# A linear-attention, routed-experts and gated-output kernel: weight sums of a later stage issued one per step over four buffers, without copies kept for the general path, and row loads ahead of weight loads

## The chip, the cores and the metric

The kernel runs on one core of a Trainium2 chip. The metric is device time in microseconds (us) of one execution; lower is better. The time of a kernel is the median of several executions. Beside it stands one profiled execution, whose trace is what the rows below are taken from. The engines are named as in the profile: PE is TensorE (matmuls, with PEld for its weight loads), DVE is VectorE, ACT is ScalarE, POOL is GpSimd, and SP issues most of the transfers (SPq is its queue).

## What is computed

The reference chains three parts, all in fp32:

```python
def _attn_ref(q, k, v, f_logit):            # (4, 8, 768, 48) each
    f = 1.0 / (1.0 + np.exp(-f_logit))
    for t in range(S):
        state = f[:, :, t, :, None] * state + np.einsum('bhd,bhe->bhde', k[:, :, t], v[:, :, t])
        y[:, :, t] = np.einsum('bhd,bhde->bhe', q[:, :, t], state)
def _moe_ref(x, expert_emb, tau, w1, w2):   # x (3072, 384), 8 experts, F = 1024
    expert_idx = np.argmax(xn @ en.T / tau, axis=1)   # xn, en: normalised rows
    gate_w = probs[np.arange(N), expert_idx]
    for e in range(E):
        h = np.maximum(x[mask] @ w1[e], 0.0)
        out[mask] = gate_w[mask, None] * (h @ w2[e])
def _moe2_ref(x, w_a, w_b, w_out):          # (384, 1536), (384, 1536), (1536, 384)
    return ((x @ w_a) * (x @ w_b) @ w_out).astype(np.float32)
```

## The kernel before

It has three stages on one core. **Attention** runs up to about 135 us: chunks of the recurrence, then the routing, which scatters each token's row into a DRAM buffer `slots`, sorted by expert. The **experts** run from there to about 404 us, the **gated output** from there to the end.

Matmuls are made of pairs: an fp32 value is split into a rounded part (hi, fp32r) and the rest (lo), and three matmuls (hi·hi, lo·hi, hi·lo) stand for one exact product. So each weight has to be split on the way: ScalarE copies the hi part, then GpSimd or VectorE subtracts it from the raw value.

**The experts' loop** has 64 steps s, 8 for each expert e (j = s % 8). A step does 128 of the 1024 hidden columns: `h_part(s)` is the first matmul (L1205 to L1207, into `ph`), then ScalarE's `hh` (L1228, relu) and VectorE's `hl` (L1229); `y_part(s - 1)` is the second matmul of the step before (L1248, into `po`), in thirds hi·`hh`, lo·`hh`, hi·`hl`. In steps j = 3, 4, 5 TensorE transposes the next expert's rows (`x_turn`, L1195, into `pt`), which come with one load from `slots` (`rows_load`, L464; for expert 1 into a tile that the trace calls `yT`, for the later ones `rows`). Raw expert weights come in pieces of 768 KB (L131 for the first ones, L879 after) and are split by `job_run`: ScalarE L887 or L893, then three subtractions of 512 columns, two on GpSimd (L896) and one on VectorE. `w_more` starts a piece when it was loaded at least `LAG_N` = 2 steps ago and its place in the ring of weights is free.

**Side work in the same steps** readies the gated stage. `prep_run(s, us)` first issues what `defer` put down for this step, then `loads()`, then as much of its streams as a budget of `us` allows (1.1 in the first eight steps, 1.8 after):

- `conv`: the weights of the gated stage, `moe2_w_a`, `moe2_w_b` (w = 0, 1) and `moe2_w_out` (w = 2), come as raw 8-byte words in 18 blocks (L926, 768 KB each, into `part` buffers 3, 4, 5 of the tile `big`). Bit operations turn each into fp32: ScalarE L949 into `ct`, then VectorE L951 to L958. Blocks of `moe2_w_out` are also split and stored in DRAM, `wost` (L970).
- `combine(w)`: for `moe2_w_a` and then `moe2_w_b`, the gated stage multiplies with 15 sums of 384 x 512 blocks' parts rather than with the weights. First three stores put the whole matrix aside in DRAM, `wkeep` (L1000), from where only the general path (`general`, taken when a flag is set, which it isn't here) reads it. Then for each of 15 sums: up to two VectorE operations (L1002, L1003); a step later ScalarE's hi (L1028) into one of nh = 3 + w buffers `hilo` and the lo (L1031) on GpSimd if the sum had operations, else on VectorE at the end of the step's side work; another step later the store into `wst` (L1047). A buffer is taken again `can` = 3 steps after its sum. Several sums of a step are possible as long as budget and buffers allow: sums 3, 3, ... at a time.
- `w_chunk`: the first three loads of `wst` back into SBUF (L1066) close the loop.

**The gated output** visits chunks of `wst` (`visit`, matmuls L1453 into `pv` and `pw`), adds the products up on VectorE (L1463, L1469), multiplies and splits (L1430, L1434, L1435) and multiplies with `w_out` (L1482 to L1486), whose blocks `wo_load` brings from `wost` (L1425) three iterations ahead. The last blocks of `moe2_w_out` are converted in this stage.

The order on each engine is the order in which the Python issues; every engine works its own list off in order. SP's list holds all the loads and stores named here, so a transfer that waits on SP holds up those behind it.

## Time and profile before

| | us |
|---|---|
| median of 3 executions (838.61 to 839.34) | 838.92 |
| the profiled execution, its own time | 843.84 |
| span of its trace, first to last instruction | 842.0 |

| engine | busy us | share of the span |
|---|---|---|
| TensorE matmul (PE) | 777.7 | 92% |
| TensorE weight load (PEld) | 743.7 | 88% |
| VectorE (DVE) | 609.2 | 72% |
| ScalarE (ACT) | 420.9 | 50% |
| GpSimd (POOL) | 392.1 | 47% |

The mean granted clock of TensorE is 0.976 of full speed; the transfers move 231.54 MB, 275 GB/s over the span. Busy time is the time in which an engine works on an instruction; the shares are means over stages with different limits, so the table of stretches below is read with them. In the rows, "idle before" in square brackets is how long an engine had nothing to do ahead of an instruction and what released it.

### The profile page before, as it was taken

How to read it: one execution, taken by the hardware profiler on the slowest of the kernel's cores; microseconds unless marked ns; L12 is line 12 of the kernel's file. 1: busy time of each engine (PE TensorE's matmuls, PEld its weight loads, DVE VectorE, ACT ScalarE, POOL GpSimd, SP SyncE). 2: the span in 40 equal slices, each digit the busy share in tenths (PEclk: the TensorE clock that was granted, in tenths of full speed). 3: DMA queues.
4: the chain of work that ended last, by engine and by line, in shares of the span. 5: the costliest groups of instructions: out<-in, count | busy, mean ns of one | idle time of the engine just before them, and what ended most of it. 6: DMA issues, size and time to landing. Idle time of an engine off the chain costs nothing. (4 is left out here: it accounts for less than half of the span.)

```text
span 842.0 us, 16799 instructions
## 1 busy us (share of the span) xinstructions
PE 777.7 (92%) x6354; PEld 743.7 (88%) x6354; DVE 609.2 (72%) x1019; ACT 420.9 (50%) x889; POOL 392.1 (47%) x380
## 2 busy tenths in 40 slices
PE   7899989599988899889878999999999999999995
PEld 5899988588887898889868999999999999999995
DVE  7999985389978767678677766756765786676552
ACT  5899963366546455374434444434433443444331
POOL 6667762253535463384044336415535343532413
PEclk9999999799999989989999999999999999999999
DMA  7989733967699885997987889889889979888982
GB/s 263 317 291 341 245 130 122 252 195 267 213 314 298 240 262 180 309 231 215 350 333 268 291 311 339 305 293 337 305 289 314 330 284 317 333 296 306 340 302 72
DMA packets 83903, 231.54 MB, mean 275 GB/s; under 512 B 10697, under 2 KB 42295, under 8 KB 77543
## 3 DMA queue, kind: packets, MB, share of 16 engines
q1 hardware_dynamic: 80455, 220.81, 78.2%
q0 software_dynamic: 3072, 9.56, 2.9%
q8 instruction: 52, 0.85, 0.4%
q14 instruction: 36, 0.29, 0.1%
q10 hardware_dynamic: 288, 0.02, 0.0%
HBM read 192.95 MB, written 37.42 MB: 274 GB/s over the span
## 5 line engine op out<-in xcount | busy, mean ns | idle before, releaser
L1435 POOL TENSOR_TENSOR w<-big,w 128x512 fp32r<-128x512 f32 x72 | 96.4, 1354 | 194.8 <-ACT w L1434 182.3
L1453 PE MATMUL pv<-w,w 128*128 128x256 f32 x912 | 136.7, 285 | 11.0 <-DVE big L1469 6.1
L1469 DVE TENSOR_TENSOR big<-big,pv 128x512 f32<-128x512 f32 x144 | 98.3, 683 | 62.5 <-PE pv L1453 62.4
L1453 PEld LDWEIGHTS pv<-w,w 128*128 128x128 f32 x912 | 127.5, 190 | 15.0 <-DVE big L1469 8.6
L1453 PE MATMUL pv<-a,w 128*128 128x256 f32 x816 | 120.6, 282 | 0.3
L1453 PEld LDWEIGHTS pv<-a,w 128*128 128x128 f32 x816 | 113.8, 189 | 2.4 <-DVE big L1469 1.2
L896 POOL TENSOR_TENSOR w<-raw,w 128x512 fp32r<-128x512 f32 x48 | 76.7, 1626 | 60.4 <-ACT w L893 56.5
L1248 PE MATMUL po<-hh,w 128*128 128x224 f32 (+7 forms) x384 | 84.0, 355 | 17.0 <-ACT hh L1228 16.4
L1486 PE MATMUL pq<-raw,w 128*128 128x384 f32 x288 | 97.6, 339 | 1.0 <-POOL w L1435 1.0
L1482 PE MATMUL pq<-raw,w 128*128 128x384 f32 x288 | 97.5, 338 | 0.0
L1484 PE MATMUL pq<-raw,w 128*128 128x384 f32 x288 | 97.1, 337 | 0.0
L1248 PEld LDWEIGHTS po<-hh,w 128*128 128x128 f32 x384 | 68.8, 196 | 20.5 <-ACT hh L1228 18.2
L1463 DVE TENSOR_TENSOR big<-big,pv 128x256 f32<-128x256 f32 x96 | 40.3, 420 | 52.9 <-PE pv L1453 49.7
L1205 PE MATMUL ph<-a,w 128*128 128x224 f32 (+7 forms) x192 | 66.9, 349 | 0.0
L1206 PE MATMUL ph<-a,w 128*128 128x224 f32 (+7 forms) x192 | 66.8, 348 | 0.0
L1207 PE MATMUL ph<-a,w 128*128 128x224 f32 (+7 forms) x192 | 66.7, 347 | 0.0
L1430 DVE TENSOR_TENSOR big<-big 128x512 f32<-128x512 f32 x72 | 64.1, 917 | 1.6
L1434 ACT ACTIVATE w<-big 128x512 fp32r<-128x512 f32 x72 | 44.8, 633 | 39.5 <-DVE big L1430 39.5
L1460 ACT ACTIVATE big<-pw 128x256 f32<-128x256 f32 x48 | 18.4, 383 | 77.8 <-PE pw L1453 77.8
L1486 PEld LDWEIGHTS pq<-raw,w 128*128 128x128 f32 x288 | 54.5, 189 | 1.6 <-POOL w L1435 1.6
L1482 PEld LDWEIGHTS pq<-raw,w 128*128 128x128 f32 x288 | 54.4, 189 | 0.3 <-ACT w L1434 0.3
L1484 PEld LDWEIGHTS pq<-raw,w 128*128 128x128 f32 x288 | 54.5, 189 | 0.0
(275 smaller groups left out, 1706.2 us busy)
## 6 DMA issues: line engine op xcount, KB each, us to landing
w<-wst SPq DMA_DIRECT2D x49, 1024.0 KB
w<-wst SPq DMA_DIRECT2D x49, 896.0 KB
raw<-wost SPq DMA_DIRECT2D x72, 384.0 KB
raw<-moe_w SPq DMA_DIRECT2D x32, 768.0 KB
qkf<-qkf SPq DMA_DIRECT2D x20, 768.0 KB
wst<-big SPq DMA_DIRECT2D x24, 512.0 KB
vx<-vx SPq DMA_DIRECT2D x24, 192.0 KB
big<-moe_w_out SPq DMA_DIRECT2D x6, 768.0 KB
```

Of the source, the lines that this page charges most:

```text
L896: (G if i < NPOOL else V).tensor_tensor(out=wt[:, 1, f], in0=raw[:, f], in1=wt[:, 0, f].bitcast(F32), op=ALU.subtract)
L1205: T.matmul(out=out, lhsT=wh, rhs=xh, start=first, stop=False)
L1206: T.matmul(out=out, lhsT=wl, rhs=xh, start=False, stop=False)
L1207: T.matmul(out=out, lhsT=wh, rhs=xl, start=False, stop=last)
L1248: T.matmul(out=OS[e][k], lhsT=w[:, j % 4, k * 128:(k + 1) * 128], rhs=x, start=(j == 0 and w is wh and x is hh), stop=(j == FJ - 1 and x i ...
L1430: V.tensor_tensor(out=a, in0=a, in1=b, op=ALU.mult)
L1435: G.tensor_tensor(out=g[:, 1], in0=a, in1=g[:, 0].bitcast(F32), op=ALU.subtract)
L1453: T.matmul(out=out, lhsT=wt, rhs=xt_, start=first and j == 0, stop=j == 2, skip_group_check=True)
L1469: V.tensor_tensor(out=o, in0=o, in1=bank, op=ALU.subtract)
L1482: T.matmul(out=q, lhsT=gh, rhs=wh, start=(f == 0), stop=False)
L1484: T.matmul(out=q, lhsT=gh, rhs=wl, start=False, stop=False)
L1486: T.matmul(out=q, lhsT=gl, rhs=wh, start=False, stop=(f == F2J - 1))
```

## The change

The text below gives the change's names; apart from the general path it touches the side work, the raw weights' lag, the order of some loads, and `wo_load`.

- No copy is kept in `wkeep`: its six stores (three for each matrix, 768 KB each) are gone. `general` recomputes the two matrices from the inputs by the same bit operations.
- `combine` has four buffers for both matrices. For the first one the fourth isn't `hilo[3]` but two pieces of `big` (columns 1024 to 1536 of each of its first two parts), and its store goes out in two cuts. A buffer is taken again after four steps. After each sum a `yield None` ends the stream's work for the step, so there is at most one sum in a step. The lo subtraction is on GpSimd for 14 of the 15 sums, on VectorE for the one without operations with i % 4 == 2 (before: 8 and 7).
- `LAG_N` is 3, the budgets are 1.4 and 2.1. The last three blocks of `conv` yield 9.0 twice in place of four times.
- The first `loads()` (three blocks of `moe2_w_out`) stands behind the first `rows_load_n(1)` and the first six `w_load()`. The rows of expert e + 2 are loaded one step later, behind `ids_store(e + 1)`.
- `wo_load` runs two iterations ahead in place of three, with two first loads in place of three.

```diff
-LAG_N = 2
+LAG_N = 3
...
                     if n >= 15:
-                        for _ in range(4):
+                        for _ in range(2):
                             yield 9.0
...
         def combine(w):
-            for k in range(KC):
-                SP.dma_start(out=wkeep[w, :, k], in_=wfs[w](k))
             blk = blocks(wfs[w])
...
-            nh = 3 + w
-            as4 = lambda t: t.rearrange("p (t c) -> p t c", t=4)
+            nh = 4
+            split4 = big[:, 0:2 * FF2].bitcast(F32R).rearrange("p (a f) -> p a f", a=2)[:, :, 1024:1536]
 
             def split(i):
-                src, to = as4(plan[i][1]), hilo[i % nh]
-                A.activation(out=to[:, :, 0], in_=src, func=ACTF.Copy)
+                src = plan[i][1]
+                if w == 0 and i % nh == 3:
+                    to = split4.rearrange("p a (b i c) -> p a b i c", b=2, i=2)
+                    hi, lo = to[:, :, :, 0], to[:, :, :, 1]
+                    src = src.rearrange("p (a b c) -> p a b c", a=2, b=2)
+                else:
+                    hi, lo = hilo[i % nh][:, :, 0], hilo[i % nh][:, :, 1]
+                    src = src.rearrange("p (t c) -> p t c", t=4)
+                A.activation(out=hi, in_=src, func=ACTF.Copy)
 
                 def low(eng):
-                    eng.tensor_tensor(out=to[:, :, 1], in0=src, in1=to[:, :, 0].bitcast(F32), op=ALU.subtract)
-
-                if plan[i][2]:
+                    eng.tensor_tensor(out=lo, in0=src, in1=hi.bitcast(F32), op=ALU.subtract)
+
+                if plan[i][2] or i % 4 != 2:
                     low(G)
                 else:
                     tail.append((0.8, lambda: low(V)))
...
-                n = 3 if w and late else 4
-                for lo, hi in ((0, n), (n, 4)):
-                    if lo < hi:
-                        dst = wst[h(lo):h(lo) + 4 * (hi - lo - 1) + 1:4, :, pos].rearrange("t p i c -> p t (i c)")
-                        SP.dma_start(out=dst, in_=src[:, lo:hi])
+                if w == 0 and i % nh == 3:
+                    cuts, tile4 = (0, 2, 4), split4.bitcast(F32).rearrange("p a (b x) -> p a b x", b=2)
+                    part4 = lambda lo, hi: tile4[:, lo // 2]
+                else:
+                    cuts = (0, 3, 4) if w and late else (0, 4)
+                    tile4 = hilo[i % nh].bitcast(F32).rearrange("p t i c -> p t (i c)")
+                    part4 = lambda lo, hi: tile4[:, lo:hi]
+                for lo, hi in zip(cuts, cuts[1:]):
+                    dst = wst[h(lo):h(lo) + 4 * (hi - lo - 1) + 1:4, :, pos].rearrange("t p i c -> p t (i c)")
+                    SP.dma_start(out=dst, in_=part4(lo, hi))
...
                 defer(1, lambda i=i: split(i))
-                can[i % nh] = now[0] + 3
+                can[i % nh] = now[0] + 4
                 yield 0.1
+                yield None
...
-        loads()
-
         running = []
...
         rows_load_n(1)
         while wstate["load"] < 6:
             w_load()
+        loads()
...
-            prep_run(s, 1.1 if s < FJ else 1.8)
+            prep_run(s, 1.4 if s < FJ else 2.1)
...
+            if j == n + 3 and e + 1 < NE:
+                ids_store(e + 1)
                 if e > 0:
                     rows_load_n(e + 2)
-            if j == n + 3 and e + 1 < NE:
-                ids_store(e + 1)
...
-                wo_load(n + 3)
+                wo_load(n + 2)
...
-        for n in range(3):
+        for n in range(2):
             wo_load(n)
```

The order of TensorE's instructions is the same in both kernels. Line numbers of the change differ a little; where the same instruction is meant, both are given.

SP's list where the experts begin, before (L464 with `yT` loads the rows of expert 1, L131 raw weights, L926 the blocks of `moe2_w_out`, L461 reads an offset from SBUF):

```order
L131 DMA raw<-moe_w 128x3x512
L926 DMA big<-moe_w_out 128x2x768 x3
L461 TENSOR_LOAD ord_i
L461 ISA x2
L464 ISA
L464 DMA yT_2535<-slots 112x1576
L131 ISA
L131 DMA raw<-moe_w 128x4x384
```

and of the change (L925, L463, L130 are the same three):

```order
L130 DMA raw<-moe_w 128x3x512
L460 TENSOR_LOAD ord_i
L460 ISA x2
L463 ISA
L463 DMA yT_2534<-slots 112x1576
L130 ISA
L130 DMA raw<-moe_w 128x4x384
L925 DMA big<-moe_w_out 128x2x768 x3
```

The three blocks of `moe2_w_out` have moved from ahead of the rows of expert 1 and a raw piece to behind them.

SP's list about the first sums of the second matrix, before (L1000 the kept copies, L879 raw pieces, L1047 the stores of sums; left out are rows loads between the two pieces):

```order
L1180 DMA heads<-ids_2541 100x40
L879 ISA
L879 DMA raw<-moe_w 128x3x512
L879 ISA
L879 DMA raw<-moe_w 128x4x384
L1000 DMA wkeep<-big 128x1536 x3
...
L1047 DMA wst<-big 128x4x256 x5
L1047 DMA wst<-big 128x3x256
```

and of the change (L878 the raw pieces, L1055 the stores of sums, L103 reads offsets):

```order
L1055 DMA wst<-big 128x4x256 x2
L878 ISA
L878 DMA raw<-moe_w 128x4x384
L1055 DMA wst<-big 128x4x256 x2
L103 TENSOR_LOAD ord_i
L103 ISA x2
L103 TENSOR_LOAD ord_i
L103 ISA x2
L878 ISA
L878 DMA raw<-moe_w 128x3x512
L1055 DMA wst<-big 128x4x256
L1055 DMA wst<-big 128x3x256
```

Pairs of raw pieces and bursts of stores have become single pieces with one or two stores between them, and the kept copies are gone.

VectorE's list in steps 58 to 61, before (L1002 a sum's operation, L1229 `hl`, L1339 and L1347 inputs of the products):

```order
L1002 TENSOR_TENSOR big<-big 128x512 x2
L1229 SCALAR_TENSOR_TENSOR hl<-ph,hh 128x384 x2
L1339 TENSOR_TENSOR rows<-yT_2534,yT_2535 128x256
L1339 TENSOR_TENSOR rows<-yT_2533,rows 128x256
L1339 TENSOR_TENSOR rows<-yT_2533 128x256
L1339 TENSOR_TENSOR rows<-rows 128x256
L1347 TENSOR_TENSOR w_66<-rows,w_66 128x256 x2
```

and of the change (L999, L1236, L1347, L1355 the same; L895 a raw piece's lo):

```order
L895 TENSOR_TENSOR w_64<-raw,w_64 128x512
L1236 SCALAR_TENSOR_TENSOR hl<-ph,hh 128x384
L999 TENSOR_TENSOR big<-big 128x512 x2
L1347 TENSOR_TENSOR rows<-yT_2533,yT_2534 128x256
L1347 TENSOR_TENSOR rows<-yT_2532,rows 128x256
L1347 TENSOR_TENSOR rows<-yT_2532 128x256
L1347 TENSOR_TENSOR rows<-rows 128x256
L1355 TENSOR_TENSOR w_66<-rows,w_66 128x256 x2
L1347 TENSOR_TENSOR rows<-yT_2532,yT_2534 128x256
L1236 SCALAR_TENSOR_TENSOR hl<-ph,hh 128x384
L999 TENSOR_TENSOR big<-big 128x512 x2
L895 TENSOR_TENSOR w_65<-raw,w_65 128x512
```

Operations of sums and subtractions of raw pieces, which came before the products' inputs, now come among them.

## Rows read from the trace of the kernel before

**Rows 1.** Stretches: length; busy us (count) of PE, PEld, DVE, ACT, POOL; clock; DMA; GB/s.

```profile
147.00:177.00 30.00, 19.11 (x147) 18.41 (x146) 15.19 (x36) 13.56 (x35) 10.23 (x9) 0.83 0.75 208
177.00:227.00 50.00, 47.21 (x233) 41.80 (x233) 47.35 (x63) 28.46 (x47) 23.53 (x15) 0.97 0.76 249
227.00:298.00 71.00, 60.85 (x316) 57.36 (x315) 54.31 (x71) 39.55 (x71) 36.24 (x24) 0.97 0.91 271
298.00:336.00 38.00, 36.03 (x197) 34.59 (x197) 27.74 (x36) 19.65 (x37) 16.57 (x11) 0.97 0.74 230
336.00:385.00 49.00, 42.57 (x233) 41.61 (x232) 37.38 (x46) 26.97 (x52) 29.81 (x19) 0.93 0.87 254
385.00:404.00 19.00, 19.00 (x110) 18.74 (x109) 14.07 (x37) 9.45 (x23) 5.51 (x2) 1.00 0.87 274
404.00:460.00 56.00, 45.17 (x309) 41.86 (x308) 41.49 (x69) 21.27 (x43) 21.02 (x17) 0.94 0.84 311
460.00:835.00 375.00, 372.80 (x2728) 368.32 (x2727) 245.76 (x406) 151.12 (x317) 154.45 (x142) 1.00 0.85 302
```

**Rows 2.** Timeline of PE: start us, us, engine, line, operation, tiles, shapes [idle before].

```profile
162.60 1.01 PE L1195 MATMUL pt<-ident,yT 112*128 112x112 f32 x4 [9.40 <-DMA yT<-slots]
165.33 0.41 PE L1205 MATMUL ph<-a,w 128*128 128x224 f32 x1
168.60 0.27 PE L1205 MATMUL ph<-a,w 128*128 128x224 f32 x1
169.60 0.55 PE L1195 MATMUL pt<-ident,yT 112*128 112x112 f32 x4
361.37 2.33 PE L1248 MATMUL po<-hh,w 128*128 128x392 f32 x6 [5.43 <-ACT hh L1228]
```

**Rows 3.** Timeline of ACT, two waits within the sums.

```profile
245.28 1.48 ACT L893 ACTIVATE w<-raw 128x1536 fp32r<-128x1536 f32 x1 [6.62 <-DMA raw<-moe_w]
356.29 0.63 ACT L1028 ACTIVATE big<-yT 128x512 fp32r<-128x512 f32 x1 [6.58 <-DMA wst<-big]
```

**Rows 4.** Waits of ACT: us in total, times, longest.

```profile
ACT big L1028 <- DMA wst<-big: 15.3, 5, 6.6
```

**Rows 5.** Two short stretches, columns as in rows 1.

```profile
160.00:170.00 10.00, 7.40 (x49) 7.40 (x49) 2.62 (x4) 3.47 (x10) 2.76 (x2) 0.64 0.73 186
236.00:240.00 4.00, 4.00 (x22) 3.85 (x21) 4.00 (x5) 2.62 (x7) 3.40 (x3) 1.00 1.02 421
```

**Rows 6.** Timeline of SP's queue and ACT at the start of the experts.

```profile
147.03 1.41 SPq L926 DMA_DIRECT2D big<-moe_w_out  x3
149.23 0.34 SPq L464 DMA_DIRECT2D yT<-slots  x1
153.49 0.88 ACT L949 ACTIVATE ct<-big 128x768 f32<-128x768 f32 x1
166.12 0.63 ACT L887 ACTIVATE w<-raw 128x512 fp32r<-128x512 f32 x1 [11.22 <-DMA raw<-moe_w]
```

**Rows 7.** Timeline of SP's queue at the first kept copies.

```profile
232.35 2.09 SPq L1000 DMA_DIRECT2D wkeep<-yT  x3
234.70 0.44 SPq L879 DMA_DIRECT2D raw<-moe_w  x1
```

**Rows 8.** Groups of POOL: shapes, count; busy us, mean ns; idle before.

```profile
L896 POOL TENSOR_TENSOR w<-raw,w 128x512 fp32r<-128x512 f32 x48 | 76.7, 1626 | 60.4 <-ACT w L893 56.5 <-PE po L1248 3.9
L1031 POOL TENSOR_TENSOR big<-big 128x512 fp32r<-128x512 f32 x6 | 9.0, 1513 | 3.4 <-ACT big L1028 3.4
```

**Rows 9.** Timeline of POOL and DVE within the sums of the second matrix.

```profile
359.69 6.80 POOL L896 TENSOR_TENSOR w<-raw,w 128x512 fp32r<-128x512 f32 x4 [1.43 <-ACT w L893]
349.24 0.68 DVE L1002 TENSOR_TENSOR big<-big 128x512 f32<-128x512 f32 x1
383.36 1.79 DVE L1002 TENSOR_TENSOR big<-big 128x512 f32<-128x512 f32 x1
```

**Rows 10.** Group of PE in the gated stage, columns as in rows 8.

```profile
L1453 PE MATMUL pv<-w,w 128*128 128x256 f32 x912 | 136.7, 285 | 11.0 <-DVE big L1469 6.1 <-DMA w<-wst 4.1 <-DVE big L1463 0.4
```

More of the change, by code (lines that the diff above doesn't have):

```diff
@@ L70, in build @@
     wost = dpool.tile([F2J, 128, 2, DM], F32, name="wost")
-    wkeep = dpool.tile([2, 128, KC, FF2], F32, name="wkeep")
     ident = const.tile([128, 128], F32, name="ident")
@@ L1040, in store @@
                 late, half, pos = AT[plan[i][0]]
-                src = hilo[i % nh].bitcast(F32).rearrange("p t i c -> p t (i c)")
                 h = lambda t: 2 * ((2 * t + w + late) % NU) + half
-                n = 3 if w and late else 4
-                for lo, hi in ((0, n), (n, 4)):
-                    if lo < hi:
-                        dst = wst[h(lo):h(lo) + 4 * (hi - lo - 1) + 1:4, :, pos].rearrange("t p i c -> p t (i c)")
-                        SP.dma_start(out=dst, in_=src[:, lo:hi])
+                if w == 0 and i % nh == 3:
[8 more added lines that the diff above has]
+                    SP.dma_start(out=dst, in_=part4(lo, hi))
             can = [0] * nh
@@ L1560, in build, with general @@
     with tc.If(fv > 0):
-        general(tc, I, out, ident, wkeep, wost, [wring[i].bitcast(F32) for i in range(6)])
+        general(tc, I, out, ident, wost, [wring[i].bitcast(F32) for i in range(6)])
     ctx.close()
-def general(tc, I, out, ident, wkeep, wost, W):
+def general(tc, I, out, ident, wost, W):
     nc = tc.nc
@@ L1653, in general @@
                for i in range(2)] for f in range(F2J)]
-        for i in range(2):
+        raw = w1.rearrange("p k f -> p (k f)").bitcast(I32)
+        ct = h.rearrange("p f c -> p (f c)")
+        r0, r1 = (raw.rearrange("p (f two) -> p f two", two=2)[:, :, i] for i in range(2))
+        for i, nm in enumerate(("moe2_w_a", "moe2_w_b")):
             for k in range(KC):
-                SP.dma_start(out=wab[i][k], in_=wkeep[i, :, k])
+                SP.dma_start(out=raw, in_=I[nm].bitcast(I32).rearrange("(k p) f -> p k f", p=128)[:, k])
+                A.activation(out=ct, in_=r1.bitcast(F32), func=ACTF.Abs)
+                V.tensor_scalar(out=ct, in0=ct, scalar1=C0, scalar2=None, op0=ALU.max)
+                V.tensor_scalar(out=ct.bitcast(I32), in0=ct.bitcast(I32), scalar1=3, scalar2=0x3fffffff,
+                                op0=ALU.logical_shift_left, op1=ALU.bitwise_and)
+                V.scalar_tensor_tensor(out=r0, in0=r0, scalar=29, in1=ct.bitcast(I32),
+                                       op0=ALU.logical_shift_right, op1=ALU.bitwise_xor)
+                V.scalar_tensor_tensor(out=ct.bitcast(I32), in0=r1, scalar=-1073741824, in1=r0,
+                                       op0=ALU.bitwise_and, op1=ALU.bitwise_xor)
+                SP.dma_start(out=wab[i][k], in_=ct)
         for f in range(F2J):
```

## The prediction

> **What bounds the kernel now.** I read first the table of stretches [rows 1]. From 460 us on TensorE is busy 372.80 of 375 us at full clock: that last part, 45% of the span, can only be shortened by taking matmuls away, and the order of TensorE is the same in both kernels, row for row. So nothing is won there. What the change touches lies before. The stretches of experts and weight sums lose, span less PE busy: 147 to 177: 10.9 us; 177 to 227: 2.8; 227 to 298: 10.2; 298 to 336: 2.0; 336 to 385: 6.4; 385 to 404: 0.0; and the start of the gated part, 404 to 460: 10.8. That is 32.3 us in the experts and 10.8 behind them.
>
> Next come the waits themselves [rows 2]. The longest in the experts are 9.40 us for the rows of expert 1 and 5.43 for `hh`, ScalarE's copy of the hidden layer; the shorter ones behind them are nearly all for `hh` too. ScalarE isn't slow: it stands in order behind something that waits. At 245.28 it is a raw weight piece that had not landed (6.62 us), at 356.29 it is a buffer of the sums that was still being stored (6.58) [rows 3], and that second kind adds up to 15.3 us in 5 waits [rows 4]. Long waits cost twice: the granted clock is 0.64 over the 10 us from 160 [rows 5], and the same matmul of 224 columns takes 0.41 us at 165.33 and 0.27 at 168.60 [rows 2]; the engine had stood still before it fell to the lower level. From the stretches' mean clocks I put this second cost at about 2 us in each of the stretches from 147, 227 and 336.
>
> So the experts are bound by TensorE with bursts of transfers on top. From 227 to 298 the DMA share is 0.91 [rows 1], and a piece of it reads 1.02, where 421 GB/s flow [rows 5]: there the transfers are the second bound, not far under the first.
>
> **The change, part by part.** I go through the same stretches. The profiled execution took 843.84 us (its span 842.0 and 1.84 around it); the median of the runs shown is 838.92, 4.92 lower. I sum what is won against the profiled execution and take it off both.
>
> *147 to 177: rows ahead of weight loads.* Before, three loads of `moe2_w_out` of 786 KB each go out at 147.03, then the rows of expert 1 (706 KB) at 149.23, then a raw piece (786 KB); TensorE gets the rows at 162.60, ScalarE the piece at 166.12 [rows 2, 6]. That is 3.85 MB in 19.1 us, 202 GB/s. In the change the rows go first, at the time of the first load now (their own wait is for the last matmul of the early part, and the queue gets past the same matmul today). They need 3.5 us at that rate, so about 150.5 to 153: step 3 reaches its transposes at about 153 and the 9.40 us go almost wholly. What is late next is ScalarE: its step 3 has the first `ct<-big` copy (L949), which found its data at 153.49 [rows 6] and now stands behind 0.706 + 0.786 + 0.786 = 2.28 MB, at 202 GB/s until 158.3. Behind it are queued two L887 copies and the copy that frees the transposes' bank, so the third set of transposes, at 169.60 before [rows 2], comes at about 158.3 + 2.7 + 0.3 = 161.3: 8.3 us earlier, the half-clock matmuls included. VectorE's bit work then starts some 3 us later against TensorE than now, which gives part back. I take 6.5, bounds 4 to 10.9.
>
> *177 to 227.* VectorE is busy 47.35 of 50 us [rows 1]; it converts the same six blocks. One raw conversion falls out of the stretch. I take 1, bounds -1 to 2.8.
>
> *227 to 298: sums of the first matrix.* Three things. (a) Three stores to `wkeep`, 128x1536 fp32 each, 2.36 MB, are gone. They went out at 232.35, and the raw piece issued behind them at 234.70 is the one that landed at 245.28 [rows 3, 7]. At the 421 GB/s of the slice just behind [rows 5] that is 5.6 us of transfers. (b) One sum a step over four buffers in place of up to three a step over three: the ScalarE copies L1028 and the stores L1047 come evenly, and the raw pieces one every second step, not two every fourth. (c) Of 15 subtractions 14 are on GpSimd and one on VectorE, where it was 8 and 7. Transfers: 0.91 of 71 us is 64.6 us, less 5.6 leaves 59; TensorE: 71 less 10.2 idle less 2 of clock leaves 59. Two bounds of the same size don't overlap perfectly, so I don't take all 12.2: I take 8, bounds 4 to 12.2.
>
> *298 to 336.* No pairs of raw pieces any more; the last three blocks of `w_b` spread over four steps. 2.0 us idle, little clock: I take 2, bounds 0 to 2.5.
>
> *336 to 385: sums of the second matrix.* The same with three more `wkeep` stores; the DMA share of 0.87 makes 42.6 us, less 5.6 is 37, well under TensorE's 40.6 (49 less 6.4 and 2). GpSimd comes near: two steps of TensorE are about 6.6 us, and hold two sums (1513 ns each) and two thirds of a raw piece (1626 ns each), 6.3 us [rows 8]. I take 5 of 8.4, bounds 0 to 8.4.
>
> *385 to 404: sums now end later.* Sums that ended at step 57 run to step 60, on the same steps in which VectorE begins the products' inputs. VectorE is busy 14.07 of 19 us here before [rows 1]. Four more sums of 0.68 to 1.79 us [rows 9] and one more raw subtraction of like size come in, nearly all in the first 6.3 us: 3.4 to 9 us on VectorE against 5 free ones spread over the whole stretch. `hl` gets late, `hh` too, since ScalarE's copies for the products wait for VectorE's sums. Queued behind: the last third of each output matmul group. The stretch has no wait now, so this is a loss: I take -3, bounds -7 to 0. The first loads of stored weights (L1066) now stand behind the last stores. The last subtraction is on GpSimd in step 60, the store goes out about step 61.3, and before the loads went out at step 61.1: no cost, unless GpSimd runs late.
>
> *404 to 460.* One load of `wost` fewer at the start, and the next block of `moe2_w_out` later: 1.2 MB less ahead of the chunks, which made TensorE wait (4.1 us in the row of L1453) [rows 10]. Against it all three last blocks are now converted here, two or so before: each is about 4 us of VectorE, and VectorE is what TensorE waits for too (6.1) [rows 10]. I take 0, bounds -4 to 4.
>
> *Costed at nothing:* `LAG_N`, the budgets of a step (they only set where the above lands, read from the order), the row loads behind the ids (used five steps later), `wo_load` two ahead (an iteration of 12 matmuls of 0.34 us each is longer than a 393 KB load at 300 GB/s, 1.3 us, and full clock and no waits from 460 on say there is room), and the general path, of which the trace has no row.
>
> Sum: 6.5 + 1 + 8 + 2 + 5 - 3 + 0 = 19.5. 843.84 - 19.5 = 824.3 for a profiled execution, 838.92 - 19.5 = **819.4** for the median.
>
> A rule that speaks against (c): the Trainium skill, page "SBUF — State Buffer", section "Who interferes with whom", says that a VectorE instruction with two SBUF inputs contends with a GpSimd instruction that reads SBUF, and that the one that starts first holds the port for its whole length. The trace agrees with a contention: the same VectorE sum takes 0.68 us at 349.24 with GpSimd idle and 1.79 at 383.36 [rows 9]. By that rule a subtraction moved to GpSimd frees VectorE of nothing; the first rival says what that would give.
>
> **The rivals.**
> 1. *GpSimd and VectorE together set the pace of the sums.* For: four raw thirds with nothing between them took 6.80 us at 359.69, 1.70 each [rows 9], and VectorE's copies of the same work stretch to 1.79 [rows 9]. If each of the four GpSimd items of two steps took 1.8 us, two steps would be 7.2 us in place of 6.6, 0.3 a step over 30 steps: 9 us less won, 828. Against: VectorE has fewer two-input instructions, and between 227 and 385 GpSimd is busy little over half [rows 1].
> 2. *Only the first wait goes.* The bursts become a steady load at the DMA bound, and the waits in the sums stay in other places: 6.5 + 1 and little else less 3, about 833. For: 59 us of transfers against 59 of TensorE. Against: 4.7 MB really go.
> 3. *More is won.* Smoothing takes nearly all waits up to 385, and the end of the sums costs nothing: 10.9 + 2 + 12 + 2 + 7 = 34, 805.
> 4. *Slower.* One mechanism: the wait of L1028 for a buffer being stored now stands in every step, ahead of `hh`, where it came five times [rows 4]. Each of the 30 sums that holds `hh` up by more than 19.5 + 3 over 30, 0.75 us, turns the gain into a loss; at 1 us each: 838.9 + 30 - 22.5 = 846. Against: a buffer is used again after four steps, about 13 us, and a store is 524 KB.
> 5. *The change doesn't act*, since the stores and loads were hidden anyway and the wait at 162.60 is for something else: 838.9.
>
> **How the numbers follow.** Forecast (811 to 826): 0.56. Rivals 1 and 2 (826 to 837): 0.24. Rival 3: 0.10. No change, within 0.2% (about what a measurement of this kernel can tell): 0.04. Slower: 0.06. The range leaves out the slower cases, no change and the outermost of 2 and 3: 804 to 835. Faster 0.90, same 0.04, slower 0.06.
>
> **What would show it.** In the profile of the changed kernel: the wait of L1195 for its rows under 1 us and one of 2 to 5 us two steps later behind the L949 copy; no granted clock under 0.9 in the sums; the stretch of the first sums 61 to 65 us; no ScalarE wait for a store above 2 us; `hl` waits of 2 to 5 us in steps 59 to 61; the first chunk there when step 64 needs it. Wrong it would be if ScalarE waits for stores in every step, if GpSimd is busy over nine tenths and TensorE waits for its output, or if TensorE waits for `w<-wst` at the start of the gated part for longer than before.

## The result and the profile after

The changed kernel takes 815.66 us (median of 4, 812.75 to 816.05) where the kernel before takes 839.13 (median of 4); the ratio is 0.9711 with a 95% interval of 0.9686 to 0.9736. That is 23.5 us less, where 19.5 were forecast (819.4). The profiled execution took 815.84 us, its span is 813.8 and its mean granted clock 0.989 (before 0.976).

The stretches of the changed kernel, cut at the same matmuls as in [rows 1] (TensorE's order is the same, so its n-th matmul marks the same place in both), with the same columns:

```profile
145.10:167.60 22.50, 17.32 (x148) 16.43 (x147) 14.95 (x36) 12.89 (x34) 8.51 (x8) 1.00 0.88 280
167.60:215.70 48.10, 46.38 (x233) 42.14 (x233) 44.02 (x64) 27.24 (x46) 19.97 (x12) 0.97 0.72 233
215.70:275.10 59.40, 57.63 (x315) 56.08 (x314) 50.26 (x59) 36.32 (x67) 45.39 (x29) 1.00 0.89 268
275.10:313.70 38.60, 35.83 (x199) 35.23 (x198) 30.09 (x40) 21.84 (x39) 18.64 (x12) 0.96 0.70 222
313.70:353.80 40.10, 40.10 (x232) 39.99 (x232) 25.66 (x37) 26.84 (x51) 33.50 (x22) 1.00 0.92 260
353.80:380.70 26.90, 20.97 (x110) 19.88 (x109) 25.04 (x42) 11.89 (x26) 18.09 (x10) 0.94 0.75 188
380.70:428.60 47.90, 42.75 (x310) 40.12 (x309) 37.14 (x65) 20.21 (x41) 18.03 (x16) 1.00 0.99 379
428.60:806.00 377.40, 373.31 (x2728) 367.64 (x2726) 250.29 (x410) 152.37 (x319) 154.77 (x141) 1.00 0.84 304
```

Read against [rows 1], first column after the bounds (the length): the first sums went from 71 to 59.4 us, the second from 49 to 40.1 with TensorE busy in all of it and full clock. The next row is the surprise: 19 us became 26.9, with VectorE busy 25.04 of them. And the row behind it gave that back: 56 became 47.9. A table by stretch, taken from the starts of the same matmuls:

| stretch of before | forecast (bounds) | gained in the trace |
|---|---|---|
| up to 147 | not looked at | 1.9 |
| 147 to 177, rows first | 6.5 (4 to 10.9) | 7.6 |
| 177 to 227 | 1 (-1 to 2.8) | 2.0 |
| 227 to 298, first sums | 8 (4 to 12.2) | 11.5 |
| 298 to 336 | 2 (0 to 2.5) | -0.6 |
| 336 to 385, second sums | 5 (0 to 8.4) | 8.9 |
| 385 to 404, sums end later | -3 (-7 to 0) | -8.0 |
| 404 to 460, gated start | 0 (-4 to 4) | 8.4 |
| 460 to the last matmul | 0 | -3.3 |

These add up to 28.4. The profiled executions are 28.0 apart and the medians 23.5, since the profiled execution of before was 4.7 above its median. A stretch also differs from one execution to the next: up to 147 us the work is the same in all the kernels below, and their traces show -0.1 to 3.6 there. And what one stretch gains the next can give back: the kernel before without its copies shows +3.6 and -4.1 in two neighbours. So the terms are tested by running, not by this table alone.

The waits of the changed kernel (us in total, times, longest), ScalarE's for transfers and TensorE's two largest:

```profile
ACT w L892 <- DMA raw<-moe_w: 1.8, 3, 1.1
ACT big L1032 <- DMA wst<-big: 1.2, 3, 0.7
PE po L1255 <- ACT hh L1235: 6.9, 3, 4.0
PE pt L1202 <- DVE a L1206: 5.4, 2, 2.8
```

ScalarE's 15.3 us for stores of sums [rows 4] are 1.2, and the 6.62 us for one raw piece [rows 3] have no successor above 1.1 in that row. The 9.40 us for the rows of expert 1 [rows 2] are gone altogether. At that place the timeline of SP's queue, ScalarE and TensorE now reads:

```profile
145.19 0.33 SPq L463 DMA_DIRECT2D yT<-slots  x1
146.28 1.72 SPq L925 DMA_DIRECT2D big<-moe_w_out  x3
154.85 0.90 ACT L948 ACTIVATE ct<-big 128x768 f32<-128x768 f32 x1 [3.16 <-DMA big<-moe_w_out]
158.78 0.60 PE L1202 MATMUL pt<-ident,yT 112*128 112x112 f32 x4 [2.67 <-DVE a L1206]
```

The rows go first, ScalarE waits 3.16 us for the block behind them, and TensorE 2.67 us at the third set of transposes.

### The profile page after: what moved, and what is told of

Read it like the earlier page. It is cut to its first block, busy times and chain, and to the rows that moved or that the text cites. A ratio compares the mean times of both kernels' runs of the same rounds, so it can differ in the third digit from the quotient of the medians.

```text
span 813.8 us, 16794 instructions
## 1 busy us (share of the span) xinstructions
PE 769.0 (95%) x6354; PEld 738.7 (91%) x6354; DVE 603.7 (74%) x1007; ACT 420.5 (52%) x889; POOL 411.6 (51%) x392
## 4 chain that ended last, share of the span: by engine, by line
PE 40%; DVE 8%; DMA 3%; issue 1%; POOL 1%; ACT 1%; SPq 0%; DVEq 0%; POOLq 0%; ACTq 0%
PE pv L1461 21%; PE pw L1461 5%; PE pq L1492 5%; PE pq L1490 5%; PE pq L1494 5%; DMA w<-wst 3%; DVE a L1355 2%; DVE big L1438 2%; DVE big L1477 2%; DVE big L1471 1%; DVE w L1355 1%; POOL out L1523 0%; POOL big L964 0%; DVE big L1474 0%; PE po L1255 0%
## 5 line engine op out<-in xcount | busy, mean ns | idle before, releaser
L1443 POOL TENSOR_TENSOR w<-big,w 128x512 fp32r<-128x512 f32 x72 | 94.2, 1322 | 173.8 <-ACT w L1442 169.6
L1461 PEld LDWEIGHTS pv<-w,w 128*128 128x128 f32 x912 | 126.3, 189 | 11.5 <-DVE big L1477 3.8
L895 POOL TENSOR_TENSOR w<-raw,w 128x512 fp32r<-128x512 f32 x48 | 78.5, 1654 | 48.1 <-ACT w L892 45.4
L1255 PE MATMUL po<-hh,w 128*128 128x224 f32 (+7 forms) x384 | 82.0, 348 | 7.4 <-ACT hh L1235 6.9
L1255 PEld LDWEIGHTS po<-hh,w 128*128 128x128 f32 x384 | 67.1, 191 | 10.1 <-ACT hh L1235 7.9
L1438 DVE TENSOR_TENSOR big<-big 128x512 f32<-128x512 f32 x72 | 66.1, 946 | 1.6
L1235 ACT ACTIVATE hh<-ph 128x224 fp32r<-128x224 f32 (+7 forms) x64 | 31.3, 490 | 52.0 <-PE ph L1214 51.8
L1494 PEld LDWEIGHTS pq<-raw,w 128*128 128x128 f32 x288 | 54.3, 189 | 2.2 <-POOL w L1443 2.2
L1490 PEld LDWEIGHTS pq<-raw,w 128*128 128x128 f32 x288 | 54.3, 189 | 0.6 <-ACT w L1442 0.6
```

Source lines behind the costliest of these rows:

```text
L895: (G if i < NPOOL else V).tensor_tensor(out=wt[:, 1, f], in0=raw[:, f], in1=wt[:, 0, f].bitcast(F32), op=ALU.subtract)
L1255: T.matmul(out=OS[e][k], lhsT=w[:, j % 4, k * 128:(k + 1) * 128], rhs=x, start=(j == 0 and w is wh and x is hh), stop=(j == FJ - 1 and x i ...
L1438: V.tensor_tensor(out=a, in0=a, in1=b, op=ALU.mult)
L1443: G.tensor_tensor(out=g[:, 1], in0=a, in1=g[:, 0].bitcast(F32), op=ALU.subtract)
L1461: T.matmul(out=out, lhsT=wt, rhs=xt_, start=first and j == 0, stop=j == 2, skip_group_check=True)
L1490: T.matmul(out=q, lhsT=gh, rhs=wh, start=(f == 0), stop=False)
```

## Experiments

Ratios are to the kernel before on the same chip; 0.001 is 0.84 us. The changed kernel has 0.9711 (0.9686 to 0.9736).

| kernel | median us | ratio (95%) |
|---|---|---|
| changed, blocks of `moe2_w_out` first again | 820.87 | 0.9773 (0.9752 to 0.9794) |
| before, rows first alone | 831.98 | 0.9938 (0.9915 to 0.9961) |
| changed, copies in `wkeep` back | 817.03 | 0.9727 (0.9706 to 0.9748) |
| before, no copies alone | 839.79 | 0.9992 (0.9973 to 1.0011) |
| changed, six subtractions a matrix back on VectorE | 812.97 | 0.9684 (0.9658 to 0.9710) |
| changed, `LAG_N` 2 | 814.09 | 0.9695 (0.9663 to 0.9727) |
| changed, all pacing undone | 833.02 | 0.9909 (0.9884 to 0.9934) |
| changed, the sums' pacing undone | 831.24 | 0.9916 (0.9894 to 0.9938) |
| changed, several sums a step | 825.43 | 0.9848 (0.9823 to 0.9873) |
| all pacing undone, one block behind the chunk loads | 826.40 | 0.9836 (0.9810 to 0.9861) |
| new: changed, inputs late | 811.52 | 0.9653 (0.9628 to 0.9677) |
| new: the same, six subtractions a matrix on VectorE, transposes ahead of the side work | 806.65 | 0.9621 (0.9591 to 0.9652) |

### Rows ahead of weight loads

Undone in the changed kernel:

```diff
         while wstate["load"] < 6:
             w_load()
-        loads()
...
+        loads()
+
         running = []
```

> The changed kernel with one part undone: the three loads of moe2_w_out go out ahead of the rows of expert 1 again. Theory (the terms of the sum add up): the wait of the transposes for these rows is back at 8 to 10 us, the half clock behind it too, and the time is up by the 7.6 us that the stretch gained in the trace: about 823. Rival (the wait only moves: the blocks are converted earlier now, and the steps behind give the time back): 816 to 819.

Measured: 0.9773, so the part is worth 0.0062, 5.2 us. TensorE's wait for the rows is back at 9.2 us, and the stretch gains 0.2 us against before in place of 7.6. From 298 to 336 the kernel without the part gains 2.0 where the changed one loses 0.6, so not all of the 7.6 is kept. The time lies between the two expectations. And the part alone, the same edit of the kernel before the other way round:

> The kernel before with one part of the change alone: the first three loads of moe2_w_out go out behind the rows of expert 1 and the raw piece. Theory (the terms add up): 840.4 less 5.2, about 835, the stretch from 147 to 177 shorter by 7 to 8 us. Rival (without the pacing the steps behind give it back): 838 to 841.

Measured: 0.9938, again 5.2 us. The term adds up: within the intervals (about 2 us either way) it is worth the same with and without everything else.

### Copies and subtractions

The six stores put back in the changed kernel, read by nothing:

```diff
+    wkeep = dpool.tile([2, 128, KC, FF2], F32, name="wkeep")
...
         def combine(w):
+            for k in range(KC):
+                SP.dma_start(out=wkeep[w, :, k], in_=wfs[w](k))
```

> The changed kernel with one part undone: the six stores to wkeep are back, and nothing reads them. Theory (transfers are the second bound in the sums): 4.7 MB at about 400 GB/s are 11 us of transfers; some 4 us of each half show, about 824. Rival (with the raw pieces coming one by one and given three steps, 5.6 us of transfers are hidden): 815 to 818.

Measured: 0.9727, 1.3 us more and within the intervals, as the rival had it. Its stretches of the first and the second sums, columns as in rows 1:

```profile
215.70:276.40 60.70, 58.12 (x316) 55.95 (x315) 50.08 (x59) 36.20 (x67) 46.45 (x29) 1.00 0.94 298
315.00:355.10 40.10, 40.10 (x233) 39.99 (x232) 25.15 (x37) 26.84 (x51) 33.37 (x23) 1.00 1.00 320
```

In the second row the transfers read 1.00 over 40.1 us, and TensorE is still busy in all 40.1: there the copies are in the transfers and not on the path. The first sums are 1.3 us longer than in the changed kernel (59.40). Taken out of the kernel before alone (which has the bursts):

> The kernel before with one part of the change alone: no copies in wkeep. Theory (the copies are hidden; with the pacing undone and the copies gone 833.0 was measured, and the row loads are worth 5.2 of that): 837 to 840. Rival (without the even pace the raw pieces stand behind the copies, and their 11 us of transfers cost 4 to 6): 832 to 836.

Measured: 0.9992, no difference that can be told; ScalarE still waits 17.0 us for stores of sums and 10.3 for raw pieces. The waits have moved, though (L1025 is L1028 of before, L892 is L893):

```profile
245.89 0.63 ACT L1025 ACTIVATE big<-yT 128x512 fp32r<-128x512 f32 x1 [3.61 <-DMA wst<-big]
318.06 1.48 ACT L892 ACTIVATE w<-raw 128x1536 fp32r<-128x1536 f32 x1 [5.11 <-DMA raw<-moe_w]
```

In the first sums no raw piece is waited for longer than 0.9 us, so the wait of 6.62 us [rows 3] went with the copies, and the stretch gains 3.6 us; behind it, in the stretch from 298, ScalarE now waits 5.11 us for a raw piece, TensorE 5.2 us for `hh`, and 4.1 us are lost. As a whole the copies cost nothing that can be told in either kernel.

The subtractions, with everything else in the same order on ScalarE and SP:

```diff
-                if plan[i][2] or i % 4 != 2:
+                if plan[i][2]:
                     low(G)
                 else:
-                    tail.append((0.8, lambda: low(V)))
+                    tail.append((0.8 if i % 4 == 2 else 0, lambda: low(V)))
```

> The changed kernel with one part undone: six of the subtractions of the sums are on VectorE again, eight on GpSimd, all else in the same order. Theory (GpSimd takes work off VectorE, which is nearly full in the sums): 2 to 5 us slower, 818 to 821. Rival (GpSimd and VectorE hold each other up, so a subtraction moved frees nothing): 814 to 817.

Measured: 0.9684, not slower and by its median 2.3 us faster, though the intervals overlap. VectorE's groups in the changed kernel (shapes, count; busy us, mean ns; idle before), L895 a raw piece's subtraction, L999 a sum, L1035 a sum's subtraction:

```profile
L895 DVE TENSOR_TENSOR w<-raw,w 128x512 fp32r<-128x512 f32 x24 | 29.1, 1213 | 7.5 <-ACT w L892 7.5
L999 DVE TENSOR_TENSOR yT<-yT,yT 128x512 f32<-128x512 f32 x10 | 12.2, 1221 | 0.1
L999 DVE TENSOR_TENSOR big<-big 128x512 f32<-128x512 f32 x10 | 11.4, 1139 | 0.1
L999 DVE TENSOR_TENSOR yT<-yT 128x512 f32<-128x512 f32 x2 | 3.0, 1480 | 0.0
L999 DVE TENSOR_TENSOR yT<-big 128x512 f32<-128x512 f32 x2 | 2.6, 1294 | 0.0
L1035 DVE TENSOR_TENSOR big<-big 128x512 fp32r<-128x512 f32 x1 | 0.7, 693 | 0.3 <-ACT big L1032 0.3
L1035 DVE TENSOR_TENSOR big<-yT,big 128x512 fp32r<-128x512 f32 x1 | 0.7, 684 | 0.0
```

and with six a matrix back on VectorE:

```profile
L895 DVE TENSOR_TENSOR w<-raw,w 128x512 fp32r<-128x512 f32 x24 | 26.7, 1112 | 8.4 <-ACT w L892 8.0
L999 DVE TENSOR_TENSOR yT<-yT,yT 128x512 f32<-128x512 f32 x10 | 9.1, 905 | 0.1
L999 DVE TENSOR_TENSOR big<-big 128x512 f32<-128x512 f32 x10 | 8.5, 846 | 0.1
L1035 DVE TENSOR_TENSOR big<-yT,big 128x512 fp32r<-128x512 f32 x7 | 7.0, 999 | 0.0
L1035 DVE TENSOR_TENSOR big<-big 128x512 fp32r<-128x512 f32 x7 | 5.9, 846 | 0.6 <-ACT big L1032 0.6
L999 DVE TENSOR_TENSOR yT<-yT 128x512 f32<-128x512 f32 x2 | 2.0, 988 | 0.0
L999 DVE TENSOR_TENSOR yT<-big 128x512 f32<-128x512 f32 x2 | 1.6, 809 | 0.0
```

Add each up: 59.7 us with 2 subtractions on VectorE, 60.8 with 14. Twelve subtractions worth 11.5 us were moved off VectorE, and the 48 other instructions became longer by 10.4. So in these groups VectorE was freed of 1.1 us, and over the whole kernel of nothing: it is busy 603.7 us in the changed kernel and 599.3 with the subtractions back. This agrees with what the Trainium skill (page "SBUF — State Buffer", section "Who interferes with whom") says: a VectorE instruction with two SBUF inputs contends with a GpSimd instruction that reads SBUF. That the first to start holds the port for its whole length, as the prediction has it, the section says of VectorE's two-port modes; no run here shows how long it is held.

### The pace

All of it undone: three buffers for the first matrix, a buffer again after three steps, several sums in a step, `LAG_N` 2, budgets 1.1 and 1.8.

```diff
-LAG_N = 3
+LAG_N = 2
...
-            nh = 4
+            nh = 3 + w
...
-                can[i % nh] = now[0] + 4
+                can[i % nh] = now[0] + 3
                 yield 0.1
-                yield None
...
-            prep_run(s, 1.4 if s < FJ else 2.1)
+            prep_run(s, 1.1 if s < FJ else 1.8)
```

> The changed kernel with the pacing undone: three buffers for the first matrix, a buffer taken again after three steps, several sums in a step, LAG_N 2, budgets 1.1 and 1.8. Theory: half of the 20.4 us that the two stretches of sums gained come from the even pace, and 8 us at the end of the experts come back, since the sums end earlier: 815 to 821, with waits of ScalarE for stores of 2 us and more. Rival (the kept copies made all of these waits, the pace none): 806 to 811, and no wait for stores above 1 us.

Measured: 0.9909, 16.6 us more than the changed kernel; both expectations were too low. The pace is by far the largest part. To divide it, first `LAG_N` alone, then the sums alone, then only the sums' bursts:

> The changed kernel with one part undone: a raw piece is split two steps after its load again, which also brings back the pairs of pieces. Theory (the pace of the sums does most of the 17 us that the pacing is worth): 817 to 820. Rival (the pieces' own waits make it: with the pacing undone ScalarE waited 13.6 us for raw pieces): 824 to 830, with these waits back.

Measured: 0.9695, no difference that can be told, and less than both expectations. As a whole pairs of raw pieces do no harm where the sums are even, though ScalarE waits 9.4 us for pieces. By the trace it is mainly two things that cancel: the sums gain less (8.4 and 7.9 us in place of 11.5 and 8.9), and the end of the experts loses 1.9 in place of 8.0.

> The changed kernel with the sums as before (three buffers for the first matrix, three steps, several in a step), while LAG_N 3 and the budgets stay. Theory (the sums' pace is the whole worth of the pacing, since LAG_N alone was worth nothing): 828 to 834, as with all of it undone. Rival (bursts of sums cost only together with pairs of raw pieces): 816 to 822.

Measured: 0.9916, as with all of it undone: beside sums in bursts `LAG_N` and the budgets are worth nothing that can be told, the sums' pace is everything.

```diff
                 can[i % nh] = now[0] + 4
                 yield 0.1
-                yield None
```

> The changed kernel with one piece of the pacing undone: several sums in a step again, while the fourth buffer, the four steps, LAG_N 3 and the budgets stay. Theory (bursts of sums make the waits): 822 to 828, with ScalarE's waits for stores back at 8 us or more. Rival (the buffers make the difference): 814 to 818.

Measured: 0.9848, 11.5 us more. The time is as the theory had it, its reason isn't. ScalarE's waits for transfers, in the kernel with all pacing undone:

```profile
ACT w L892 <- DMA raw<-moe_w: 13.6, 5, 7.0
ACT big L1032 <- DMA wst<-big: 12.8, 4, 5.3
```

with the sums' pacing undone:

```profile
ACT big L1032 <- DMA wst<-big: 17.6, 8, 4.2
ACT w L892 <- DMA raw<-moe_w: 2.6, 2, 1.8
```

and with several sums a step over the four buffers:

```profile
ACT w L892 <- DMA raw<-moe_w: 12.7, 7, 4.5
ACT big L1032 <- DMA wst<-big: 0.8, 1, 0.8
```

Four buffers and four steps remove the waits for stores (17.6 to 0.8); one sum a step removes the waits for raw pieces (12.7 to 1.8). A likely reason is in SP's lists shown ahead of the prediction, where raw loads stand among bursts of stores; it was not tested by itself. It takes both to have neither. In the first sums the trace shows 11.5 us gained with both, 7.3 with the buffers alone, 2.2 with neither; in the second 8.9, 7.0 and -1.5. So in the sums the buffers do most; what one sum a step adds lies mainly at the gated start.

### The gated start

SP's queue in the kernel before (L970 stores into `wost`, L1066 the chunk loads; a load of a block of `moe2_w_out`, L926, goes out at 412.35 between the two):

```profile
410.45 1.80 SPq L970 DMA_DIRECT2D wost<-big  x2
413.94 0.58 SPq L1066 DMA_DIRECT2D w<-wst  x1
```

With all pacing undone the stretch from 404 gains 1.0 us, not 8.4. SP's queue there, and the wait of TensorE behind it (L1074 the chunk loads, L969 stores into `wost`, L925 a block of `moe2_w_out`):

```profile
400.81 0.32 SPq L1074 DMA_DIRECT2D w<-wst  x1
401.87 2.38 SPq L969 DMA_DIRECT2D wost<-big  x2
404.31 0.55 SPq L925 DMA_DIRECT2D big<-moe_w_out  x1
404.95 13.79 SPq L1074 DMA_DIRECT2D w<-wst  x4
413.65 2.93 PE L1460 MATMUL pv<-w,w 128*128 128x256 f32 x12 [4.52 <-DMA w<-wst]
```

and in the changed kernel (L1075 the chunk loads):

```profile
384.93 14.47 SPq L1075 DMA_DIRECT2D w<-wst  x5
399.49 2.08 SPq L969 DMA_DIRECT2D wost<-big  x2
```

With the pacing undone, the store of a converted block, which waits for that block to be split, and the next block's load stand ahead of four chunk loads; in the changed kernel the conversion begins later, since the sums end later, and five chunk loads go out ahead of them. The later block alone, brought into the kernel with all pacing undone:

```diff
-            phase[0] = 4
             while now[0] <= NE * FJ - 4:
                 yield None
             for h in range(3):
                 w_chunk(h)
+            while now[0] < NE * FJ + -1:
+                yield None
+            phase[0] = 4
```

> The kernel with the pacing undone (833.0), and in it the block of moe2_w_out that goes out ahead of the first chunk loads goes out three steps later, behind them, so that SP's order at the start of the gated part is that of the changed kernel: five chunk loads, then the store into wost. Theory (the start of the gated part gains since no store that waits for its split stands ahead of the chunk loads on SP; the pacing brings that order about by ending later): the wait of 4.5 us for w<-wst and the half clock behind it go, 824 to 827. Rival (the gain has another cause, such as VectorE's work being laid out otherwise): 831 to 834.

Measured: 0.9836 against 0.9909, 6.1 us less. The same queue now:

```profile
397.65 13.63 SPq L1074 DMA_DIRECT2D w<-wst  x5
411.38 2.08 SPq L969 DMA_DIRECT2D wost<-big  x2
```

TensorE has no wait for `w<-wst` left, and the stretch gains 10.2 us. The edit moves the block as a whole: its load, its conversion on ScalarE and VectorE, and its store. TensorE's waits for VectorE in the stretch fall too, from 5.1 to 2.0 us. So the block's place is shown to be worth 6.1 us; that SP's order does it is supported by the wait of 4.52 that went, but VectorE's work being laid out otherwise, the rival, isn't ruled out.

Two other kernels say that the queue isn't all. With several sums a step the stretch gains -0.7 us, and most of that kernel's 11.5 us lie here; stores and a block load do stand ahead of four chunk loads, but TensorE waits 2.6 us for `w<-wst` and 9.0 for VectorE's adding up (L1470, L1476). With the sums' pacing undone the store is out before the first of four chunk loads is due, TensorE waits 0.9 us for `w<-wst`, and the stretch still gains only 1.6.

In the change itself the waits point mostly to VectorE. The group of [rows 10] in the changed kernel:

```profile
L1461 PE MATMUL pv<-w,w 128*128 128x256 f32 x912 | 135.6, 283 | 7.0 <-DMA w<-wst 2.4 <-DVE big L1471 1.5 <-DVE big L1477 1.3
```

The waits for chunks went from 4.1 to 2.4 us; those for VectorE in the stretch went from 6.6 to 1.3. VectorE is busy 37.14 us there in place of 41.49, and one conversion has left the stretch: the first operation of the last three blocks starts at 404.2, 423.0 and 444.9 before, and at 391.5, 410.3 and 430.6 in the changed kernel, whose stretch ends at 428.6. With fewer waits the clock is 1.00 there in place of 0.94, and the same matmuls take 42.75 us in place of 45.17 [rows 1]. No run tests this apart from the queue.

### The end of the experts, and two new versions

The loss of 8.0 us, in the changed kernel's timeline (VectorE, ScalarE, TensorE; L1347 the sums of the products' inputs, L1360 their hi copies, L1235 `hh`):

```profile
356.81 3.01 DVE L999 TENSOR_TENSOR big<-big 128x512 f32<-128x512 f32 x2
359.75 1.51 DVE L1347 TENSOR_TENSOR rows<-yT,yT 128x256 f32<-128x256 f32 x1
361.75 0.42 ACT L1360 ACTIVATE w<-rows 128x256 fp32r<-128x256 f32 x1 [4.32 <-DVE rows L1347]
363.69 1.32 PE L1255 MATMUL po<-hh,w 128*128 128x384 f32 x6 [1.90 <-ACT hh L1235]
364.14 2.39 DVE L999 TENSOR_TENSOR big<-big 128x512 f32<-128x512 f32 x2
366.45 1.76 DVE L895 TENSOR_TENSOR w<-raw,w 128x512 fp32r<-128x512 f32 x1
369.98 0.42 ACT L1360 ACTIVATE w<-rows 128x256 fp32r<-128x256 f32 x1 [4.14 <-DVE rows L1347]
371.14 1.15 PE L1255 MATMUL po<-hh,w 128*128 128x384 f32 x5 [4.03 <-ACT hh L1235]
```

VectorE's sums and a raw subtraction, at 1.2 to 1.8 us each, come ahead of the input's sum; ScalarE's copy of that input waits for it, 4.32 and 4.14 us; `hh`, behind the copy in ScalarE's order, keeps TensorE waiting 1.90 and 4.03. These 5.9 us are one part of the loss. The other is the clock, 0.94 in the stretch in place of 1.00: the same matmuls take 20.97 us in place of 19.00 [rows 1]. The first new version does the inputs late:

```diff
             if s > IDS:
-                for _ in range(3):
+                for _ in range((1, 1, 2, 3, 4, 5)[s - IDS - 1]):
                     next(x_first, None)
```

> A new version: the changed kernel with the subtractions divided between GpSimd and VectorE as before (813.0), and the inputs of the products prepared with 1, 1, 2, 3, 4, 5 parts in the last six steps in place of 3 in each. Theory (the 9 us lost at the end of the experts are ScalarE's hh standing behind copies that wait for VectorE): most of the waits for hh there go, 805 to 809. Rival (the work comes all the same, and the first products wait for it): 812 to 816.

The expectation describes more than was run: this kernel has only the inputs late, and 14 of 15 subtractions still on GpSimd. So it is to be read against the changed kernel.

Measured: 0.9653, 4.9 us less than the changed kernel and clear of it. The waits for `hh` there fall to 0.42, and one of 1.64 for `hl` stays; the stretch loses 4.4 in place of 8.0, with the clock at 0.93. So about half of that loss came back. The second new version takes on the wait for the transposes' bank (5.4 us in 2 places above), and also has the six subtractions a matrix on VectorE, by the same edit as above:

```diff
+            if 3 <= j <= 5:
+                x_turn(e + 1, j - 3)
             prep_run(s, 1.4 if s < FJ else 2.1)
             w_more(s)
             if 1 <= s <= 3:
                 next(count_ops)
-            if 3 <= j <= 5:
-                x_turn(e + 1, j - 3)
```

> A new version: that with the products' inputs prepared late (811.5), and in steps j = 3, 4, 5 the transposes of the next expert's rows with their copies ahead of the side work. Theory (TensorE waits 5.7 us in two places for the copy that frees the transposes' bank, which stands behind the side work on VectorE): 805 to 809. Rival (VectorE now waits for the transposes and the side work ends later): 811 to 816.

Measured: 0.9621 (0.9591 to 0.9652), 806.65 us. The wait for the transposes' bank is no longer among TensorE's longer ones. Against the first version (0.9653) the intervals overlap, and two edits lie between the two, so the transposes' own share isn't shown; against the changed kernel the three edits together are 7.6 us faster, clear of both intervals.

## Why the prediction was right, and where it was not

The time was right within 4 us. Of its reasons these held, and these not.

- **Rows first: right.** 6.5 forecast, 7.6 in the trace, 5.2 by undoing it and by doing it alone. The wait for the rows is 0, the one forecast two steps later is 2.67 us (2 to 5 said), and the clock of the stretch is 1.00 in place of 0.83. What it waits for is VectorE's half of the copy that frees the bank (L1206), which comes late behind the block's conversion; ScalarE had the block at 154.85, not at the 158.3 worked out from 202 GB/s.
- **The sums: the right place and, in size, on the high side of the range, but with a wrong cause among three.** 13 us were taken for the two stretches, and the trace shows 20.4 (the first came out at 59.4 us where 61 to 65 was the sign given). Step (a), 5.6 us of transfers for each matrix's copies, is what failed: it read a DMA share of 0.91 [rows 1] as a bound, and took the copies off it. With the copies back the share of the second sums is 1.00, and TensorE waits for nothing there. The raw piece that was late at 245.28 [rows 3] was late behind the copies, as (a) had it, since the wait went with them; but without them another piece was late one stretch on, and nothing was won. Step (b), the even pace, is nearly the whole gain: with the sums' pacing undone the two stretches gain 0.7 us. Step (c), GpSimd, is no gain: the rule weighed in the prediction was right, and rival 1 named the place; its price of 9 us was too high: 2.3 us by the medians, and the intervals don't tell that from nothing.
- **The end of the experts: the mechanism right, the size not.** The bound was -7, taken -3, and it was -8.0. Five more instructions came to VectorE, as counted, but it is busy 11.0 us more where 3.4 to 9 were taken: the sums and subtractions cost 1.2 to 1.8 us each here, near the upper end of the 0.68 to 1.79 [rows 9], and the products' inputs became longer too. That GpSimd beside them makes them long isn't shown at this place: with the subtractions back on VectorE the stretch loses 9.0. The term also had no clock in it, which is 2 of the 8.0 us. And the loss went through ScalarE to `hh`, which was named, not through waits of 2 to 5 us for `hl`, which were the sign given.
- **The gated start: wrong.** Costed at 0 (-4 to 4), it gained 8.4. Two steps failed. The count of conversions had it the wrong way round, three blocks in the stretch where two or so were before: three were in it before and two are after, and the waits for VectorE fell from 6.6 to 1.3 us. And the step counted bytes, and didn't look at what stands ahead of the chunk loads on SP; moving one block behind them was worth 6.1 us in the kernel with all pacing undone. The end's error (5.0 us worse than taken) and this one (8.4 better) are of opposite sign; that they cancel in part is luck, and the sum is nearer than its terms.
- **From 298 to 336, and from 460:** 2 and 0 were taken, -0.6 and -3.3 came. The first has a 2.8 us wait for the transposes' bank, which is gone in the second new version (there the stretch gains 1.5; with its subtractions alone it gains 0.3). Of the second some 2 us lie between 438.6 and 450 of the changed kernel: TensorE waits there for VectorE's adding up, 1.0 and 0.6 us, just behind the conversion that left the stretch before. The rest of it was not traced to a cause. The 1.9 us before 147 weren't either: the work there is the same in all kernels here, and their traces show -0.1 to 3.6, so it is put down to one execution differing from another.
- **Rival 4, slower:** a wait for a store in every step did not come; the longest is 0.7 us.

Left open: whether the six subtractions on VectorE gain 2 us or nothing; what the transposes ahead of the side work gain by themselves; how the 16.6 us of the pace divide between waits in the sums and the gated start; and how much of the gated start is SP's order and how much VectorE's.

## What to carry to other kernels

Side work that feeds an engine in order should come at an even pace, with as many buffers as the steps until a buffer is free again (four here); bursts made both the buffers and the loads late here. A high share of busy transfers is no bound by itself: look for the one transfer that is waited for, and at what stands ahead of it in its queue, such as a store whose data isn't there yet; and when a wait goes, look whether it has only moved to the next stretch. Count which work falls into a stretch before and after, and not only how much of it there is. Moving two-input vector work to GpSimd is to be priced with what it adds to the vector work that stays.

## What the runs showed of the hardware

In the second sums with the copies back, transfers at a share of 1.00 and 320 GB/s over 40.1 us left TensorE busy in all of them. Twelve subtractions of 128x512 moved from VectorE to GpSimd freed VectorE of 1.1 us of the 11.5 they had taken in the groups shown, as the instructions that stayed became longer: the two large groups of sums went from 0.91 and 0.85 us to 1.22 and 1.14, the raw pieces' subtractions from 1.11 to 1.21.
